# Scaling V by a sum of squares, joint tails of a head pair, and the rescaling of x as planned GpSimd work

## The chip, the cores and the metric

The kernel runs on one core of a Trainium2 chip. The metric is the device time of one execution in microseconds: 1048.24 us is the median of three runs of the kernel before (1047.64 to 1049.55). A core has a matmul engine (TensorE, PE in the profile), three engines for elementwise work (VectorE = DVE, ScalarE = ACT, GpSimd = POOL), and a queue that issues DMAs (SyncE = SP). Each engine executes its instructions in the order in which they stand, and waits at one whose inputs or buffers are not ready.

## The reference

Three stages follow each other. The first is causal attention with a decay, over 4 batches, 8 heads, 576 positions and a head size of 64:

```python
scores = scale * np.matmul(q, k.transpose(0, 1, 3, 2))
cum = np.cumsum(np.log(np.clip(f, 0.0001, 1.0)), axis=-1)
decay = cum[:, :, :, None] - cum[:, :, None, :]
scores = np.where(causal, -1000000000.0, scores + decay)
attn = np.exp(scores - np.max(scores, axis=-1, keepdims=True))
attn = attn / (np.sum(attn, axis=-1, keepdims=True) + 1e-09)
attn_out = np.matmul(attn, v)
x = attn_out.transpose(0, 2, 1, 3).reshape(B * S, H * D)   # 2304 x 512
a, b = x @ w_a, x @ w_b                                    # 512 -> 1536
x = a * b @ w_out                                          # 1536 -> 512
h = x @ w_in                                               # 512 -> 2048
g = np.where(h >= 1, h, np.where(h <= -1, 0.0, (h + 1) ** 2 / 4))
return g @ moe2_w_out                                      # 2048 -> 512
```

All inputs and the output are float32.

## The kernel before

Float32 products are built from half-precision pieces. A matrix is scaled by a power of two and split into a high and a low fp16 part (`xh`/`xl` for the activations, `whi`/`wlo` for weights, `vh`/`vl` for V), and a product is three fp16 matmuls (`mm3`, L589 to L591 in the profile). The scale has to keep the high part in range, so each tensor that is split first has its largest magnitude found: a reduction along the row, a transpose on PE, a maximum over the row, masking to the exponent (`top_of`), and a small matmul that spreads the result to all partitions (`spread`).

The program has two phases. **The first phase** is attention for all 16 pairs of heads, with the first group of the second layer for batches 0 to 2 between its steps. It goes in rounds, seven for each pair: score matmuls (`s`), mask and row minimum on DVE (`prob`, `nm`), Exp on ACT, transposes on PE (`tp`), a split of the probabilities on ACT (`th`) and DVE (`tl`), and matmuls with V (`o`). The 576 queries of a head are four blocks of 128 and a tail of 64. Both heads' tails are computed together, in one round, with head 0 on partitions 0 to 63 and head 1 on 64 to 127. At the end of a head its result is divided by its row sum (`z`) and written to `xt`, and at the end of a batch `xpose` transposes `xt` and splits it into `xh` and `xl`.

V of a pair is loaded (`load_v`, tile `vraw`), its largest magnitude per head is found on DVE (`v_max`, tile `mx`), the scales of a group of up to four pairs are spread to `scs` (`v_scale`), and V is scaled and split (`v_split`: ACT writes `vh`, POOL scales `vraw` in place and writes `vl`). Because `o` is V's scale times the result, the row sum is multiplied by it too.

`xh` and `xl` of batch b are written with the smallest V scale known by then, `xsc[:, b]`. When the last V scale is known, batches 0 to 2 are brought to `xsc[:, 3]` by `rescale(b)`: a ratio and eight multiplications of 576 columns, on DVE (L1087 and L1091). They may not run before the matmuls of the second layer's first group have read the batch.

The instructions of the first phase are not issued at once. `Plan` records them with their dependencies, gives each a duration by a table (`cost`), and puts them in order by a list schedule: at each step the engine that can start first takes the ready operation of highest rank, and the ranks come from 20 sweeps forward and backward. Where PE would idle in that plan, matmuls on a constant tile are put in (L1097, `mm<-mask`), which do no work. The recorded operations are then issued, all from L305, with their order kept.

**The second phase** (all lines but L305 in the profile) is the rest of both layers. It is written after the plan in program order, and the framework's own scheduler may put its instructions on an engine between those of the plan. `xpose(3)` and `rescale(0..2)` belong to it. Weights are loaded in 68 units, decoded on ACT, DVE and POOL, and split ahead of their use.

## Time and profile before

| | value |
|---|---|
| median of three runs | 1048.24 us (1047.64 to 1049.55) |
| profiled execution | 1044.85 us, its span 1043.1 us |
| PE busy | 1010.7 us (97%), 6871 matmuls |
| DVE busy | 736.0 us (71%) |
| ACT busy | 600.4 us (58%) |
| POOL busy | 584.7 us (56%) |
| mean granted clock of PE | 0.990 |

The shares are means over both phases, so they say little of either. A stretch of the trace is read from a table of windows: for each, its length, the busy time of PE, of PE's weight loads, DVE, ACT and POOL with the number of instructions in brackets, the clock that PE was granted as a share of the full 2.4 GHz, the busy share of the DMA engines and GB/s. Matmuls overlap each other, so PE's busy time is not its work. The chain of waits goes back from the last instruction to what released each; its rows have a start, a length, an engine, the tile that is written and the line. A row of a group of operations has, after the bar, the busy time in total, the mean of one in ns, and the idle time of the engine just before them with what ended it. An operation of the first phase is told by its tile, since all have line 305.

### The profile page before, as it was taken

To read this page: it belongs to the slowest core of one execution; us is meant where nothing else is said; L and a number is where in the kernel's file an instruction comes from. 1 tells how busy PE (TensorE), PEld (TensorE's weight loads), DVE (VectorE), ACT (ScalarE), POOL (GpSimd) and SP (SyncE) were. 2 spreads that over 40 slices of the span, in tenths; PEclk is the share of its full clock that TensorE was granted. 3 is DMA by queue.
4 is the path that set the end of the run, shared out by engine and by line. 5 is a ranking of instruction groups with operands and counts; after the bars stand their busy time and mean duration, and the time that the engine had idled before them with its cause. 6 is when DMAs were issued, how large, how long until landed. Compare 5 with 4: busy or idle time off the path is not lost.

```text
span 1043.1 us, 18612 instructions
## 1 busy us (share of the span) xinstructions
PE 1010.7 (97%) x6871; PEld 594.1 (57%) x6871; DVE 736.0 (71%) x1761; ACT 600.4 (58%) x1159; POOL 584.7 (56%) x635
## 2 busy tenths in 40 slices
PE   7999999799899999999999999999999999999998
PEld 6787788678764544455454444445554454455554
DVE  7999999887878774564663777984378767744443
ACT  4899788677765444352543445676666546535342
POOL 6698868565177644352553446785377546725221
PEclk8999999899999999999999999999999999999999
DMA  8663544331033121111120211111012102000112
GB/s 248 176 194 113 161 144 134 108 96 54 2 102 98 48 77 41 41 41 41 41 81 1 81 41 41 41 41 41 1 43 80 41 14 68 1 1 1 66 45 74
DMA packets 22060, 72.06 MB, mean 69 GB/s; under 512 B 2776, under 2 KB 5336, under 8 KB 21904
## 3 DMA queue, kind: packets, MB, share of 16 engines
q1 hardware_dynamic: 21968, 70.87, 22.7%
q8 instruction: 54, 0.88, 0.4%
q14 instruction: 38, 0.31, 0.1%
HBM read 60.26 MB, written 5.96 MB: 63 GB/s over the span
## 4 chain that ended last, share of the span: by engine, by line
PE 70%; DVE 19%; ACT 3%; POOL 3%; issue 3%; DMA 2%; SPq 0%; DVEq 0%; ACTq 0%; POOLq 0%
PE mm L589 21%; PE mm L590 20%; PE mm L591 20%; DVE prob L305 3%; DVE tl L305 3%; PE s L305 2%; PE mm L305 2%; PE tp L305 2%; PE o L305 1%; DMA vraw<-in_v_dram 1%; DVE xt L305 1%; DVE xhl L1091 1%; DVE xhl L741 1%; DVE wm L305 1%; DMA y<-y 1%
## 5 line engine op out<-in xcount | busy, mean ns | idle before, releaser
L640 POOL TENSOR_TENSOR al<-tmp 128x460 f16<-128x460 f32 (+2 forms) x134 | 159.7, 1193 | 192.7 <-ACT tmp L637 183.5
L589 PE MATMUL mm<-xhl,whi_in 128*128 128x460 f16 (+2 forms) x752 | 266.4, 355 | 1.2 <-DVE tmp L776 1.2
L591 PE MATMUL mm<-xhl,wlo_in 128*128 128x460 f16 (+2 forms) x752 | 266.5, 355 | 0.0
L590 PE MATMUL mm<-xhl,whi_in 128*128 128x460 f16 (+2 forms) x752 | 266.5, 355 | 0.0
L590 PE MATMUL mm<-al,wdown 128*128 128x460 f16 (+2 forms) x536 | 190.1, 356 | 1.0 <-POOL al L640 1.0
L591 PE MATMUL mm<-ah,wlo_out 128*128 128x460 f16 (+2 forms) x536 | 190.1, 356 | 0.0
L589 PE MATMUL mm<-ah,whi_out 128*128 128x460 f16 (+2 forms) x536 | 178.8, 356 | 0.5 <-DVE tmp L776 0.5
L636 ACT ACTIVATE ah<-tmp 128x460 f16<-128x460 f32 (+2 forms) x134 | 77.7, 580 | 107.2 <-DVE tmp L776 49.4
L590 PEld LDWEIGHTS <-whi_in 128*128 128x128 f16 x752 | 73.6, 98 | 69.5 <-issue 2.0
L591 PEld LDWEIGHTS <-wlo_in 128*128 128x128 f16 x752 | 73.5, 98 | 69.5
L589 PEld LDWEIGHTS <-whi_in 128*128 128x128 f16 x752 | 73.5, 98 | 68.6 <-issue 0.2
L775 ACT ACTIVATE tmp<-tmp,hmid,ihalf 128x460 f32<-128x460 f32 (+1 forms) x80 | 60.9, 761 | 76.6 <-DVE tmp L774 76.5
L518 POOL TENSOR_TENSOR wm<-wm,wr 128x512 int32<-128x512 int32 x58 | 75.8, 1307 | 50.8 <-DVE wm L515 42.6
L776 DVE SCALAR_TENSOR_TENSOR tmp<-mm,hfull,tmp 128x460 f32<-128x460 f32 (+1 forms) x80 | 55.6, 694 | 60.6 <-ACT tmp L775 56.7
L305 ACT ACTIVATE prob<-prob,nm 128x384 f32<-128x384 f32 (+4 forms) x144 | 80.7, 583 | 16.8 <-DVE nm L305 16.1
L591 PEld LDWEIGHTS <-wlo_out 128*128 128x128 f16 x536 | 52.4, 98 | 51.7 <-issue 1.8
L686 DVE SCALAR_TENSOR_TENSOR tmp<-mm,gr,tmp 128x460 f32<-128x460 f32 (+2 forms) x54 | 36.7, 679 | 63.5 <-PE mm L591 56.4
L590 PEld LDWEIGHTS <-wdown 128*128 128x128 f16 x536 | 52.4, 98 | 50.4 <-issue 0.9
L589 PEld LDWEIGHTS <-whi_out 128*128 128x128 f16 x536 | 52.4, 98 | 49.8
L774 DVE TENSOR_SCALAR tmp<-mm,htop,hlow 128x460 f32<-128x460 f32 (+1 forms) x80 | 59.9, 749 | 28.0 <-PE mm L591 26.5
L637 ACT ACTIVATE tmp<-ah 128x460 f32<-128x460 f16 (+2 forms) x134 | 77.6, 579 | 3.0
L725 DVE SCALAR_TENSOR_TENSOR y<-mm,os,y 128x460 f32<-128x460 f32 (+1 forms) x100 | 64.8, 688 | 20.0 <-PE mm L591 19.9
(185 smaller groups left out, 2115.4 us busy)
## 6 DMA issues: line engine op xcount, KB each, us to landing
wraw<-in_w_dram SPq DMA_DIRECT2D x68, 512.0 KB
raw<-in_qk_dram SPq DMA_DIRECT2D x26, 608.0 KB
vraw<-in_v_dram SPq DMA_DIRECT2D x16, 320.0 KB
qk<-q SPq DMA_DIRECT2D x28, 160.0 KB
out_dram<-tmp SPq DMA_DIRECT2D x16, 230.0 KB
cum_d<-xhl SPq DMA_DIRECT2D x1, 1216.0 KB
y<-in_qk_dram SPq DMA_DIRECT2D x2, 608.0 KB
out_dram<-tmp SPq DMA_DIRECT2D x4, 232.0 KB
```

The lines of the kernel that those rows point to most:

```text
L305: getattr(getattr(self.nc, engine), method)(*a, **kw)
L518: nc.gpsimd.tensor_tensor(t, t, r, ALU.add)
L589: nc.tensor.matmul(o, lhsT=wh, rhs=xh, start=first, stop=False)
L590: nc.tensor.matmul(o, lhsT=wd, rhs=xl, start=False, stop=False)
L591: nc.tensor.matmul(o, lhsT=wl, rhs=xh, start=False, stop=last)
L636: nc.scalar.activation(ah, r, AF.Copy, scale=1.0 / LOW)
L637: nc.scalar.activation(spare, ah, AF.Copy, scale=LOW)
L640: after(delay + 1, lambda: nc.gpsimd.tensor_tensor(al, r, spare, ALU.subtract))
L725: nc.vector.scalar_tensor_tensor(ys, o, sc, ys, ALU.mult, ALU.add)
L774: nc.vector.tensor_scalar(t, o, top[:, m], low[:, m], ALU.min, ALU.max)
L775: after(1, lambda: nc.scalar.activation(t, t, AF.Square, scale=ihalf[:, m], bias=mid))
L776: after(2, lambda: nc.vector.scalar_tensor_tensor(r, o, full[:, m], t, ALU.mult, ALU.max))
```

## The change

**V's bound.** `v_max` is one Square on ACT over both heads of a pair, with the sum of the squares of each row as a second output, instead of a maximum on DVE for each head. The square root of a sum of squares is at least the largest magnitude. `top_of` takes the root of the exponent by a shift, which is one more short DVE operation. There is one scale for a pair, so `scs` has half as many columns, `v_split` takes one operation on ACT and one on POOL for both heads, and two constants of the second layer's scales change by a factor of two.

**Tails.** A pair's tail has one operation for `z`, one reciprocal and one multiplication over 128 partitions, since both heads share a scale, and it is written to columns of `xt` that belong to the pair. `xpose` brings it back with 64-column matmuls against halves of the identity into one tile, and splits it in one operation on each engine instead of two. `xt` needs no zeros.

**Rescaling.** `rescale` runs on POOL, is recorded in the plan with everything else, and so its place is chosen by the list schedule. The smallest scale is found in `xscale`.

The core of the diff:

```diff
@@ top_of
+        if squares:
+            nc.vector.tensor_scalar(m2i[0:n], m2i[0:n], 1, 0x3F800000, ALU.logical_shift_right, ALU.bitwise_and)
+            nc.vector.tensor_scalar(m2[0:n], m2[0:n], 2.0 ** 63, None, ALU.mult)
+        else:
+            nc.vector.tensor_scalar(m2i[0:n], m2i[0:n], 0x7F800000, None, ALU.bitwise_and)
@@ v_max
-            vst["mx", p0] = sm_p.tile([P, 2 * NPAIR], F32, name="mx", tag="mx")
-        mx = vst["mx", p0][:, 2 * (pp - p0):2 * (pp - p0) + 2]
-        nc.vector.tensor_reduce(mx, vraws[pp].rearrange("p a c d -> p a (c d)"), axis=AX.X, op=ALU.max,
-                                apply_absolute_value=True)
+            vst["mx", p0] = sm_p.tile([P, NPAIR], F32, name="mx", tag="mx")
+        mx = vst["mx", p0][:, pp - p0:pp - p0 + 1]
+        nc.scalar.activation(junk, vraws[pp].rearrange("p a c d -> p (a c d)"), AF.Square, accum_out=mx)
@@ v_split
-        for a in range(2):
-            nc.scalar.activation(vh[:, a, :, 0:D], t[:, a], AF.Copy, scale=sc[:, a:a + 1])
-            nc.gpsimd.tensor_scalar(t[:, a], t[:, a], sc[:, a:a + 1], 0.0, ALU.mult, ALU.add)
+        nc.scalar.activation(vh[:, :, :, 0:D], t, AF.Copy, scale=sc)
+        nc.gpsimd.tensor_scalar(t, t, sc, 0.0, ALU.mult, ALU.add)
@@ pv_step, the tail of a pair
-            for i in range(2):
-                rows = slice(i * TAIL, (i + 1) * TAIL)
-                nc.vector.tensor_scalar(z[rows], o[rows, D:D + 1], PSC * 1e-9, sc[rows, i:i + 1], ALU.add, ALU.mult)
+            nc.vector.tensor_scalar(z, o[:, D:D + 1], PSC * 1e-9, sc, ALU.add, ALU.mult)
             nc.vector.reciprocal(z, z)
-            for i in range(2):
-                rows = slice(i * TAIL, (i + 1) * TAIL)
-                h = (2 * pp + i) % H
-                nc.vector.tensor_scalar(xt[rows, NCH - 1, h * D:(h + 1) * D], o[rows, 0:D], z[rows], None, ALU.mult)
+            p = pp % NPAIR
+            nc.vector.tensor_scalar(xt[:, NCH - 1, p * D:(p + 1) * D], o[:, 0:D], z, None, ALU.mult)
@@ xpose, the tails
         for kc in range(KC):
-            nc.tensor.transpose(tp[:, kc * P:(kc + 1) * P], xt[:, NCH - 1, kc * P:(kc + 1) * P], ident)
...
+            for i in range(2):
+                rows = slice(i * TAIL, (i + 1) * TAIL)
+                nc.tensor.matmul(tv[rows, kc, :], lhsT=xt[:, NCH - 1, kc * D:(kc + 1) * D], rhs=ident[:, rows], start=True, stop=True)
+        nc.scalar.activation(h[:, :, 512:576], tv, AF.Copy, scale=sb)
+        nc.vector.scalar_tensor_tensor(l[:, :, 512:576], tv, sb, h[:, :, 512:576], ALU.mult, ALU.subtract)
@@ rescale
-        nc.vector.tensor_tensor(r, xsc[:, B - 1:B], xinv[:, b:b + 1], ALU.mult)
+        nc.gpsimd.tensor_tensor(r, xsc[:, B - 1:B], xinv[:, b:b + 1], ALU.mult)
...
-                nc.vector.tensor_scalar(o, o, r, None, ALU.mult)
+                nc.gpsimd.tensor_scalar(o, o, r, 0.0, ALU.mult, ALU.add)
@@ main program, before the plan is ordered and issued
+    xscale(B - 1)
+    for b in range(B - 1):
+        rescale(b)
     with tc.manual_schedule():
         nc.issue()
@@ main program, second phase
-    for b in range(B - 1):
-        after(6 + 8 * b, lambda b=b: rescale(b))
```

Since the list schedule sets the order, the change moves instructions throughout the first phase. Three places are shown, in the built programs' own order.

On ACT at the start, the small operation `wdg` (a diagonal of the first V scale, for the matmul that spreads it) stands in the kernel before ahead of all work on the tables of cumulative sums (`xhl<-y`) and on weights (`wm`, `wr`):

```order
L305 ACTIVATE xt<-xt 64x576
L305 ACTIVATE wdg_152<-ident,w_0_151 2x2
L305 ACTIVATE vh_136<-vraw_148,scs 128x5x64 x2
L305 ACTIVATE wm_186<-wraw_184 128x512
L305 ACTIVATE wr_187<-wraw_184 128x512
L305 CAST xhl<-y 64x1216 x2
L305 ACTIVATE wm_186<-wraw_185 128x512
```

Now the Square (`junk`, `mx`) comes behind the logarithm, and `wdg` stands behind four operations that were after it:

```order
L305 ACTIVATE xt<-xt 64x576
L305 ACTIVATE junk,mx_150<-vraw_149 128x640
L305 CAST xhl<-y 64x1216
L305 ACTIVATE wm_187<-wraw_185 128x512
L305 CAST xhl<-y 64x1216
L305 ACTIVATE wr_188<-wraw_185 128x512
L305 ACTIVATE wdg_153<-ident,w_0_152 1x1
L305 ACTIVATE wm_187<-wraw_186 128x512
```

The matmul that waits for `wdg` has moved in PE's order as well: 29 of 98 matmuls on the constant tile stood ahead of it at the start, and now 50 of 146.

On DVE, where the last V scale has become known, two ratios and the first eight rescales stand in the kernel before between operations of attention (`z` and `xt` are the end of a pair's tail, `tl` the low part of probabilities, `ISA prob` the mask with the row minimum):

```order
L1087 TENSOR_TENSOR ratio_4633<-xsc,xinv 128x1
L1087 TENSOR_TENSOR ratio_4694<-xsc,xinv 128x1
L305 TENSOR_SCALAR z_0_182<-o_169,scs 64x1 x2
L305 ISA prob_133,nm_181<-s_159,mask 128x128
L305 ISA nm_181 128x1
L1091 TENSOR_SCALAR xhl<-xhl,ratio_4633 128x576 x5
L305 RECIPROCAL z_0_182<-z_0_182 128x1
L305 SCALAR_TENSOR_TENSOR tl_168<-tp_150,th_167 128x384
L1091 TENSOR_SCALAR xhl<-xhl,ratio_4633 128x576 x3
L305 TENSOR_SCALAR xt<-o_169,z_0_182 64x64 x2
L305 SCALAR_TENSOR_TENSOR tl_179<-tp_160,th_178 128x512
```

At the same place, the smallest scale, DVE now has only its reduction and reciprocal:

```order
L305 SCALAR_TENSOR_TENSOR tl_169<-tp_151,th_168 128x384
L305 TENSOR_SCALAR z_0_183<-o_170,scs 128x1
L305 SCALAR_TENSOR_TENSOR tl_180<-tp_161,th_179 128x512
L305 RECIPROCAL z_0_183<-z_0_183 128x1
L305 TENSOR_REDUCE xsc<-scs 128x1
L305 TENSOR_SCALAR ot_228<-ot_228 128x1
L305 TENSOR_SCALAR xt<-o_170,z_0_183 128x64
L305 TENSOR_SCALAR os_229<-winv,ot_228 128x2
L305 ISA prob_133,nm_166<-s_160,mask 128x320
L305 ISA nm_166 128x1
L305 RECIPROCAL xinv<-xsc 128x1
```

On POOL, in the stretch between the preparations of two heads (`k`, `q` and `qk` are the copy and the splits of a head, `al` the low part of the second layer's product), the kernel before has no rescale:

```order
L305 TENSOR_TENSOR al_208<-tmp_206,tmp_205 128x288
L305 TENSOR_SCALAR vraw_189<-vraw_189,scs 128x320
L305 TENSOR_SCALAR k_2_130<-raw_156 128x576
L305 TENSOR_TENSOR qk_2_131<-raw_156,k_2_130 64x576
L305 TENSOR_TENSOR q_2_129<-raw_156,q_2_129 64x640
L305 TENSOR_SCALAR vraw_189<-vraw_189,scs 128x320
```

In the changed kernel the longest run of rescales stands there:

```order
L305 TENSOR_TENSOR al_209<-tmp_207,tmp_206 128x288
L305 TENSOR_TENSOR qk_1_129<-raw_175,k_1_128 64x576
L305 TENSOR_SCALAR xhl<-xhl,ratio_230 128x576 x5
L305 TENSOR_SCALAR xhl<-xhl,ratio_231 128x576
L305 TENSOR_TENSOR ratio_230<-xsc,xinv 128x1
L305 TENSOR_SCALAR xhl<-xhl,ratio_231 128x576 x5
L305 TENSOR_TENSOR al_213<-tmp_211,tmp_210 128x288
L305 TENSOR_SCALAR k_2_131<-raw_157 128x576
L305 TENSOR_TENSOR q_2_130<-raw_157,q_2_130 64x640
```

Five more rescales are spread over rows ahead of these, and the last eight stand behind the last `qk` of the phase. From the last recorded operation on, the order of POOL and SP is that of the kernel before but for four places on POOL.

## Rows read from the trace of the kernel before

**Rows 1.** Windows: us, busy (count) of PE, PEld, DVE, ACT, POOL, clock, DMA, GB/s

```profile
18.00:30.00 12.00, 12.00 (x48) 8.29 (x48) 7.03 (x23) 7.64 (x14) 2.55 (x2) 0.57 0.84 246
30.00:180.00 150.00, 144.07 (x1755) 119.77 (x1752) 145.83 (x494) 130.99 (x281) 121.17 (x116) 1.00 0.52 151
180.00:210.00 30.00, 24.45 (x283) 20.69 (x282) 26.11 (x81) 20.85 (x45) 19.20 (x18) 0.89 0.37 113
210.00:220.00 10.00, 7.77 (x54) 6.00 (x53) 10.00 (x28) 7.06 (x16) 5.11 (x6) 0.83 0.27 80
220.00:258.00 38.00, 37.16 (x454) 30.77 (x453) 28.91 (x93) 29.91 (x65) 23.61 (x23) 1.00 0.28 77
345.00:600.00 255.00, 255.00 (x1317) 127.45 (x1315) 150.46 (x272) 107.80 (x200) 117.74 (x106) 1.00 0.17 50
```

**Rows 2.** Chain of waits, 182 to 215 us: start us, us, what

```profile
182.52 0.92 DVE ratio L1087 x2
184.13 2.17 DVE xhl L1091 x5
186.82 3.31 DVE xhl L1091 x3
...
212.69 1.88 DVE xhl L1091 x3
```

**Rows 3.** Waits of PE, 178 to 224 us: total us, times, longest us

```profile
PE o L305 <- DVE xt L305: 3.3, 1, 3.3
```

**Rows 4.** Groups of operations, DVE: busy us, mean ns, idle us before

```profile
L305 DVE TENSOR_REDUCE mx<-vraw 128x2 f32<-128x640 f32 x16 | 12.9, 809 | 3.7 <-DMA vraw<-in_v_dram 3.7
...
L1091 DVE TENSOR_SCALAR xhl<-xhl,ratio 128x576 f16<-128x576 f16 x24 | 11.9, 538 | 0.0
...
L305 DVE TENSOR_SCALAR xt<-o,z 64x64 f32<-64x64 f32 x32 | 9.0, 280 | 0.4
...
L305 DVE TENSOR_SCALAR z<-o,scs 64x1 f32<-64x1 f32 x32 | 6.9, 215 | 1.9 <-PE o L305 1.5
...
L305 DVE SCALAR_TENSOR_TENSOR xhl<-tp,xsc,xhl 64x256 f16<-64x256 f32 x6 | 2.9, 482 | 0.8 <-ACT xhl L305 0.7
...
L1087 DVE TENSOR_TENSOR ratio<-xsc,xinv 128x1 f32<-128x1 f32 x3 | 1.1, 406 | 0.0
```

**Rows 5.** Timeline of PE, 6 to 25 us: start us, us

```profile
6.62 6.79 PE L1097 MATMUL mm<-mask 128*128 128x224 bf16 x69
17.83 6.47 PE L305 MATMUL s<-y 66*128 66x128 f32 x14 [4.43 <-DMA y<-y]
```

**Rows 6.** Timeline of ACT, 8 to 11 us

```profile
8.18 0.68 ACT L305 ACTIVATE wm<-wraw 128x512 f32<-128x512 f32 x1
...
9.31 1.20 ACT L305 CAST xhl<-y 64x1216 fp32r<-64x1216 f32 x1
```

**Rows 7.** Groups of operations, ACT

```profile
L305 ACT CAST q<-raw 128x640 fp32r<-128x640 f32 x26 | 18.7, 721 | 1.7 <-PE s L305 1.4 <-DMA raw<-in_qk_dram 0.2
L305 ACT ACTIVATE vh<-vraw,scs 128x320 f16<-128x320 f32 x32 | 17.7, 559 | 1.8 <-DVE scs L305 1.4 <-PE o L305 0.4
...
L305 ACT ACT_TABLE_LOAD x2 | 2.6, 1283 | 0.8 <-PEq L1226 0.7
```

**Rows 8.** Groups of operations, POOL

```profile
L305 POOL TENSOR_SCALAR vraw<-vraw,scs 128x320 f32<-128x320 f32 x32 | 18.5, 579 | 27.2 <-ACT vh L305 24.1 <-PE tp L305 2.7
L305 POOL TENSOR_SCALAR k<-raw 128x576 fp32r<-128x576 f32 x26 | 18.4, 707 | 22.4 <-PE s L305 14.7 <-issue 7.2 <-POOL q L305 0.4
```

**Rows 9.** Line 1091: duration ns min/median/max, first and last start us

```profile
L1091 DVE TENSOR_SCALAR xhl<-xhl,ratio x24: 351/361/1637, 184.0 to 265.4; 128x576 f16<-128x576 f16 x24
```

**Rows 10.** Window 205 to 262 us

```profile
205.00:262.00 57.00, 53.93 (x608) 44.52 (x607) 47.62 (x150) 44.18 (x95) 32.57 (x30) 0.97 0.27 76
```

**Rows 11.** Timeline of POOL, 281 us, with the idle time before

```profile
281.06 1.36 POOL L532 TENSOR_SCALAR wm<-wm,wsc 128x512 f32<-128x512 f32 x2 [13.64 <-ACT whi_in L531]
```

**Rows 12.** Timeline of PE, 265 us

```profile
265.57 0.93 PE L305 MATMUL tp<-ident,prob 128*128 128x128 f32 x7
```

More of the change, by code (lines that the diff above doesn't have):

```diff
@@ L377, in tile_decay_attention__then__moe__then__moe2 @@
     winv = const.tile([P, NU], F32, name="winv")
-    scs = const.tile([P, B * H], F32, name="scs")
+    scs = const.tile([P, B * NPAIR], F32, name="scs")
+    junk = const.tile([P, 2 * NCH * D], F16, name="junk")
     xsc = const.tile([P, B], F32, name="xsc")
@@ L449, in constants @@
             nc.gpsimd.memset(V(t[64:P, :]), 0.0)
-        nc.gpsimd.memset(xt[:, NCH - 1, :], 0.0)
     def set_of(hh):
@@ L470, in slot, with top_of @@
         return slots[k][split[k] - 1]
-    def top_of(mx, n):
+    def top_of(mx, n, squares=False):
         tp = psum_t()
@@ L660, in out_scale1 @@
             nc.vector.tensor_scalar(t, group1(g)[0], xinv[:, b:b + 1], 2.0 ** 31, ALU.mult, ALU.mult)
-            nc.vector.tensor_scalar(t[:, 0:1], t[:, 0:1], t[:, 1:2], 2.0, ALU.mult, ALU.mult)
+            nc.vector.tensor_scalar(t[:, 0:1], t[:, 0:1], t[:, 1:2], 4.0, ALU.mult, ALU.mult)
             nc.vector.tensor_scalar(o, winv[:, u:u + 2], t[:, 0:1], None, ALU.mult)
@@ L882, in v_scale @@
             return
-        n = 2 * (p1 - p0)
+        n = p1 - p0
         mx = vst.pop(("mx", p0))[:, 0:n]
-        spread(top_of(mx, n), n, None, scs[:, 2 * p0:2 * p1])
+        spread(top_of(mx, n, True), n, None, scs[:, p0:p1])
     def v_split(pp):
-        t, sc = vraws.pop(pp), scs[:, 2 * pp:2 * pp + 2]
+        t, sc = vraws.pop(pp), scs[:, pp:pp + 1]
         vh, vl = vhs[pp % 2], vls[pp % 2]
-        for a in range(2):
-            nc.scalar.activation(vh[:, a, :, 0:D], t[:, a], AF.Copy, scale=sc[:, a:a + 1])
-            nc.gpsimd.tensor_scalar(t[:, a], t[:, a], sc[:, a:a + 1], 0.0, ALU.mult, ALU.add)
+        nc.scalar.activation(vh[:, :, :, 0:D], t, AF.Copy, scale=sc)
+        nc.gpsimd.tensor_scalar(t, t, sc, 0.0, ALU.mult, ALU.add)
         nc.gpsimd.tensor_tensor(vl, t, vh[:, :, :, 0:D], ALU.subtract)
@@ L995, in pv_step @@
                 z = sm_p.tile([P, NCH - 1], F32, name="z", tag="z")
-                nc.vector.tensor_scalar(z, o[:, :, D], PSC * 1e-9, sc[:, a:a + 1], ALU.add, ALU.mult)
+                nc.vector.tensor_scalar(z, o[:, :, D], PSC * 1e-9, sc, ALU.add, ALU.mult)
                 nc.vector.reciprocal(z, z)
@@ L1060, in round_step, with xscale @@
             pv_step(k - OFF[2])
+    def xscale(b):
+        sb = xsc[:, b:b + 1]
+        nc.vector.tensor_reduce(sb, scs[:, 0:NPAIR * (b + 1)], axis=AX.X, op=ALU.min)
+        nc.vector.reciprocal(xinv[:, b:b + 1], sb)
     def xpose(b):
         sb = xsc[:, b:b + 1]
-        nc.vector.tensor_reduce(sb, scs[:, 0:H * (b + 1)], axis=AX.X, op=ALU.min)
-        nc.vector.reciprocal(xinv[:, b:b + 1], sb)
         h, l = (a[:, :, b * S:(b + 1) * S] for a in (xh, xl))
@@ L1073, in xpose @@
         tp = psum_t()
+        tv = tp[:, 0:KC * TAIL].rearrange("p (k t) -> p k t", k=KC)
         for kc in range(KC):
-            nc.tensor.transpose(tp[:, kc * P:(kc + 1) * P], xt[:, NCH - 1, kc * P:(kc + 1) * P], ident)
-        tv = tp.rearrange("p (k t) -> p k t", k=KC)
-        for i in range(2):
-            rows = slice(i * D, (i + 1) * D)
-            cols = slice(i * TAIL, (i + 1) * TAIL)
-            nc.scalar.activation(h[rows, :, 512:576], tv[rows, :, cols], AF.Copy, scale=sb[rows])
-            nc.vector.scalar_tensor_tensor(l[rows, :, 512:576], tv[rows, :, cols], sb[rows], h[rows, :, 512:576],
-                                           ALU.mult, ALU.subtract)
+            for i in range(2):
[3 more added lines that the diff above has]
+        nc.vector.scalar_tensor_tensor(l[:, :, 512:576], tv, sb, h[:, :, 512:576], ALU.mult, ALU.subtract)
     def rescale(b):
         r = const2.tile([P, 1], F32, name="ratio", tag="ratio")
-        nc.vector.tensor_tensor(r, xsc[:, B - 1:B], xinv[:, b:b + 1], ALU.mult)
+        nc.gpsimd.tensor_tensor(r, xsc[:, B - 1:B], xinv[:, b:b + 1], ALU.mult)
         for a in (xh, xl):
@@ L1138, in tile_decay_attention__then__moe__then__moe2 @@
             if k // RB < B:
+                xscale(k // RB - 1)
                 xpose(k // RB - 1)
```

3 lines of the change are left out of this document (1 added, 2 removed).

## The prediction

> **What bounds the kernel now.** I read the table of stages first, then the chain of waits through the stage that loses most, then who PE waited for there, then the durations of the operations that the change touches. The reader is to see three things.
>
> First, from 345 us on PE is busy all the time (255.00 of 255 us in [rows 1]). The second phase is matmul work, 438 POOL rows and 77 SP rows follow the last planned row in both orders, and they differ in four places and in none. So what the change is worth is what it moves the end of the first phase by, at about 281 us; everything behind shifts along.
>
> Second, in the first phase DVE is the engine that is never free: 145.83 of 150 us from 30 to 180 us, and 10.00 of 10 from 210 to 220, where ACT has 130.99 of 150 and POOL 121.17. PE is "busy" 144.07 there, but its matmuls overlap, so that is no proof of a full engine.
>
> Third, the worst places are two blocks of rescaling on DVE. They belong to the second phase, but stand in DVE's queue in the middle of the first. The chain of waits runs through two ratios (0.92 us), then five and three rescales (2.17 and 3.31 us) before it comes back to PE, and again at 212 us [rows 2]. PE waited 3.3 us in one piece for the DVE operation behind the first block [rows 3]. After that wait the granted clock is down: 0.89 of full speed on average from 180 to 210 us, 0.83 from 210 to 220, against 1.00 before and after [rows 1].
>
> **Term A, the rescaling leaves DVE.** In the order of the changed kernel no rescale stands on DVE; all 24 are on POOL, in places that the list schedule chose. What this block cost is read on PE: from 180 to 210 us it was idle for 30 - 24.45 = 5.55 us, and at 0.89 of the clock lost 24.45 x 0.11 = 2.7 us; from 210 to 220 us, 10 - 7.77 = 2.23 us and 7.77 x 0.17 = 1.3 us. Sum 11.8 us, and I take all of it: A = -11.8. The ends: 0, if what was late behind DVE is late behind POOL instead; and -18, if DVE itself is the limit (24 x 538 ns = 12.9 us [rows 4], 1.1 us of ratios, 4.0 us of clock).
>
> **Term B, the start.** PE ran out of filler matmuls at 13.4 us (69 of them in 6.79 us, 0.098 us each) and stood still for 4.43 us until the rows with the cumulative sums had landed at 17.83 us [rows 5]. From 18 to 30 us the clock was 0.57, near the lower of its two levels (1.2 GHz), with PE busy throughout: 12 x 0.43 = 5.2 us of work lost [rows 1]. The new order has 146 fillers ahead of the first score matmul instead of 98 (27, 23 and 96 instead of 21, 8 and 69), so the wait is covered and the clock should stay up. But they may end too late: the small matmul that the last 96 follow now waits for an ACT operation that stands behind two casts of 1.20 us and two decoding operations of 0.68 us [rows 6], so it comes at about 6.6 + 3.8 = 10.4 us, and 96 x 0.098 = 9.4 us more end at 19.8, 2.0 us after the data. (The same loads stand ahead of those rows in SP's queue, in another order, so I leave 17.8 us.) B lies between -5.2 and +2.0; their sum is -3.2, and as DVE was busy for 7.03 us of that stage and the steps of a round wait for each other, I take -2.0.
>
> **Term C, the rest of DVE's relief.** The maxima go to ACT: 11 of the 16 stand behind the start, 11 x 809 ns = 8.9 us. The tails of a pair are scaled in one operation instead of two: 16 x 215 ns = 3.4 us and 16 x 280 ns = 4.5 us; three of six splits of transposed tails go, 1.4 us [rows 4]. Added is one short operation in each of five scale groups, at most 5 x 215 ns = 1.1 us. That frees 17.1 us of an engine that is 97% busy. What PE can make of it is less: it idles for 5.93 us from 30 to 180 us, and runs 81 fillers there (7.9 us), so 13.8 us at most, and nothing if ACT is next. The order has 48 fillers behind the start instead of 85; 37 x 0.098 = 3.6 us is my value: C = -3.6.
>
> **Term D, what is added.** ACT: 16 squares over 640 columns with a sum; no row shows one with a sum. Bounds: not below the 721 ns of a 640-column cast, not above two 320-column operations (1118 ns) [rows 7]. I take 721, the row of the same width, so 7.9 us for the 11 behind the start. Joining 32 scalings of 320 columns (17.9 us) into 16 of 640, between 721 and 1118 ns, at 830 ns gives 4.6 back, and three splits of tails 1.4. Net ACT +2 us. POOL: 24 rescales of 576 columns. The nearest row is the copy of k, as wide, at 707 ns [rows 8]: 17.0 us; joining the scalings of V gives some 5 back; net +12 us. Its ends are the 351 ns of the same operation on DVE and its 1637 ns at worst [rows 9]. What hides it: POOL idles for 57 - 32.57 = 24.4 us from 205 to 262 us [rows 10], where 16 of them go (11.3 us), and for 13.64 us before 281 us [rows 11], where the last eight go (5.7 us). If that cover fails, all 12 us and ACT's 2 us are on the path. PE: 32 matmuls of 64 columns for 16 transposes; the spacing of transposes is 0.93 / 7 = 0.13 us [rows 12], so between 0 (half as long each) and +2.1 us; I take 1.0. Of the 14 us on ACT and POOL I let 2 show, since queues are in order and the plan's gaps are not the chip's. D = +3.0, between 0 and +16.
>
> The rows say that a rescale is twice as long on POOL (707 against a median of 361 ns). The Trainium skill says the same more strongly: VectorE: DVE Perf Modes, Rules for kernel authors, wants 16-bit operations with a scalar from and to SBUF on VectorE for its fastest mode, and GPSIMD Engine Reference, Engine selection, sends elementwise work to VectorE. By that rule the move costs 24 x 0.346 = 8.3 us of engine time and the sum would be -14.4 + 8.3 = -6.1; by the chain of waits, DVE's time at that place is the dear one. No row of this kernel shows a rescale on POOL.
>
> **The sum.** -11.8 - 2.0 - 3.6 + 3.0 = -14.4 us. The profiled execution took 1044.85 us (span 1043.1), so 1030.45; the median of the runs, 1048.24, is 3.39 above that execution, which gives 1033.8, rounded to 1034.
>
> **Rivals.**
> 1. Half of it comes back (20%). The block's place on the chain is taken by POOL's preparation of the next head or by ACT. For it: behind 220 us POOL, ACT and PE are all between 62 and 98% busy and DVE is no longer full (28.91 of 38) [rows 1]. Against it: the wait of 3.3 us and the clock behind it have no other cause in the rows. A halves to -5.9, B is 0, C halves to -1.8, D stays: -4.7, so 1043.5.
> 2. Slower (9%). The list schedule puts 11 rescales and a ratio in one run on POOL, ahead of a subtraction for the second layer and of the copy and splits of the next head. If they take 1.10 us each, as the three did on DVE while POOL worked (3.31 / 3 [rows 2]), and if score matmuls wait for all 16, that is 17.6 us on the chain, and PE's idling would take the clock down again for 4.0 us: -11.8 - 2.0 - 3.6 + 1.0 + 21.6 = +5.2, so 1053.4. It decides from 16.4 us of such delay on. For it: POOL releases q and k for PE. Against it: 24.4 us of idle time in that very stretch. GPSIMD Engine Reference, Key points, in the Trainium skill, states that GpSimd shares its SBUF interfaces with VectorE and contends with some of its instructions; the spread of 351 to 1637 ns on DVE agrees [rows 9].
> 3. Larger (13%). DVE's 97% was the true limit of the whole first phase and the start keeps its clock without delay: -11.8 - 5.2 - 10 + 2.0 = -25, so 1023.2. For it: no other engine is as full from 30 to 180 us. Against it: PE and ACT have only 6 and 19 us of slack there [rows 1].
> 4. It doesn't do what it says (3%): Square needs another table than Exp and each group of maxima loads two. ACT_TABLE_LOAD takes 1283 ns [rows 7]; five groups make 12.8 us and eat the gain, near 1047. The order has two such loads in both kernels, so this is nearly excluded.
>
> The forecast itself holds 55%, with a range of its own from 1027 to 1040.
>
> **The numbers.** A difference of 0.2% (2.1 us, below 1046.1 or above 1050.4) is what a measurement of this kernel can tell. Faster: the forecast, rival 3 and most of rival 1, 85%. Within: the rest of rival 1 and rival 4, 5%. Slower: rival 2 with a little for what I haven't seen, 10%. The range from 1020 to 1046 covers the forecast, rivals 1 and 3 but for their outer ends, and leaves out rivals 2 and 4.
>
> **What would show it.** Right: PE idles for under 2 us between 175 and 215 us and its clock stays at 1.00 there; from 18 to 30 us the clock is well above 0.57; the first score matmul starts between 17.5 and 20 us; DVE is busy for about 700 instead of 736 us, POOL for about 597, ACT for about 603; the first phase ends near 267 us. Wrong: PE or ACT waits in pieces of 2 us or more for POOL's copy or splits of q and k while rescales run; a rescale takes over 1.1 us; or the first phase ends earlier but PE then waits for weights before 345 us, so that the gain is given back.

## The result and the profile after

The changed kernel takes 1034.74 us (median of four runs, 1033.59 to 1035.86), the kernel before, in the same session, 1048.89 us (1047.64 to 1049.72). The ratio is 0.986, its 95% interval 0.982 to 0.990. The profiled execution took 1033.59 us, its span is 1031.8 us, 11.3 us less than that of before. Runs over 1.5% above the fastest of the same kernel are left out of the ratios here and below, which concerns one of the 11 with the longer filler (1051.57 us) and two of the 13 of the kernel before beside the first group.

The windows of the changed kernel, same columns as [rows 1] and with the same stretches but the first of 18 to 30 us:

```profile
18.00:30.00 12.00, 12.00 (x93) 10.29 (x92) 4.48 (x14) 6.49 (x13) 1.39 (x3) 1.00 0.84 231
30.00:180.00 150.00, 142.04 (x1751) 116.97 (x1750) 139.79 (x477) 136.19 (x297) 123.99 (x108) 0.99 0.54 163
180.00:210.00 30.00, 29.97 (x359) 25.45 (x357) 22.74 (x79) 24.37 (x53) 22.98 (x25) 1.00 0.37 110
210.00:220.00 10.00, 9.89 (x122) 7.91 (x121) 5.63 (x22) 7.32 (x18) 9.84 (x12) 1.00 0.44 145
345.00:600.00 255.00, 253.73 (x1309) 126.64 (x1307) 148.29 (x274) 107.59 (x201) 116.68 (x106) 1.00 0.15 46
```

From 180 to 220 us PE idles for 0.14 us where it idled for 7.78, at full clock; this is what term A said. From 18 to 30 us the clock is 1.00 instead of 0.57. From 30 to 180 us ACT now has 136.19 of 150 us where it had 130.99, and DVE 139.79 where it had 145.83, but PE is not busier. In the second phase PE misses 1.27 us of 255 that it didn't miss before; the one wait listed there is for ACT:

```profile
PE mm L593 <- ACT ah L640: 1.3, 1, 1.3
```

PE's waits from 178 to 224 us, where [rows 3] had 3.3 us, are down to one short one. In the chain of waits (start, length, engine, tile) PE follows PE where [rows 2] went through ratios and the first rescales. From 210.8 to 215.7 us, where [rows 2] had the second block, the chain goes through ACT, but PE lost little by it (9.89 of 10 us busy from 210 to 220 us). The wait first, then two stretches of the chain:

```profile
PE tp L305 <- DVE w L305: 0.3, 1, 0.3
```

```profile
182.28 0.60 PE o L305 x30
182.88 0.84 PE mm L305 x6
183.72 1.40 PE s L305 x11
185.61 0.91 PE o L305 x30
...
210.79 0.71 ACT q L305
...
214.50 0.79 ACT prob L305 x2
```

The rescales on POOL, the joined scaling of V, and on ACT the Square with the instruction that reads its sum (busy us, mean ns, idle before), beside [rows 4, 7, 8]:

```profile
L305 POOL TENSOR_SCALAR xhl<-xhl,ratio 128x576 f16<-128x576 f16 x24 | 17.5, 742 | 2.7 <-PE mm L305 2.7
L305 POOL TENSOR_SCALAR vraw<-vraw,scs 128x640 f32<-128x640 f32 x16 | 13.7, 855 | 17.0 <-ACT vh L305 9.5 <-issue 3.6 <-DVE nm L305 3.3
L305 ACT ACTIVATE vh<-vraw,scs 128x640 f16<-128x640 f32 x16 | 13.3, 833 | 0.9 <-PE o L305 0.6 <-POOL al L305 0.2
L305 ACT ACTIVATE junk<-vraw 128x640 f16<-128x640 f32 x16 | 11.8, 736 | 3.4 <-DMA vraw<-in_v_dram 3.4
...
L305 ACT ACTIVATION_READ_ACCUMULATOR junk<-vraw 128x1 f32 x16 | 3.1, 196 | 0.0
```

A rescale takes 742 ns on POOL (707 was taken), and at most 747. The Square takes 736 ns as the row of a cast said, but an instruction of its own reads the sum for another 196 ns.

PE's start, beside [rows 5]:

```profile
1.47 5.18 PE L1096 MATMUL mm<-mask 128*128 128x224 bf16 x27 [1.47 <-DVE mm L1095]
...
12.52 0.16 PE L305 MATMUL tp<-wdg,ones 1*128 1x1 bf16 x1 [3.56 <-ACT wdg L305]
12.61 11.03 PE L1096 MATMUL mm<-mask 128*128 128x224 bf16 x96
23.48 2.99 PE L305 MATMUL s<-y 66*128 66x512 f32 x12
```

The first score matmul starts at 23.48 us, 5.65 us later than before and behind the 17.5 to 20 of the forecast, for two reasons. The small matmul on `wdg` came at 12.5 us instead of 10.4, as ACT waited 2.28 us for POOL and 0.96 us for DVE ahead of its two casts. And after PE's wait of 3.56 us the clock fell to 0.50, so the 96 fillers took 11.03 us instead of 9.4 (the first row is a window of 2.5 us, the second of 2):

```profile
13.50:16.00 2.50, 2.50 (x15) 1.98 (x14) 2.06 (x4) 1.08 (x3) 2.07 (x3) 0.50 1.06 231
16.00:18.00 2.00, 2.00 (x19) 1.82 (x18) 0.00 (x0) 1.22 (x3) 2.00 (x3) 0.82 0.98 213
```

In the execution without rescaling, with the same order of PE, `wdg` came at 11.41 us, the 96 fillers took 9.37 us and the first score matmul started at 20.71 us.

How far each execution had come is read from matmuls issued by a time, those on the constant tile left out. I worked them out from windows that begin at 0, once of all and once of that tile. Executions with the same first phase can be compared row by row; the two kernels differ by a few small matmuls per batch and in the order of the others, so across them the counts are rough. "None" is without the rescaling, "twice" with each rescale issued twice.

| matmuls issued by (us) | 30 | 60 | 120 | 180 | 220 | 280 |
|---|---|---|---|---|---|---|
| before | 50 | 400 | 1011 | 1719 | 2052 | 2747 |
| changed | 35 | 396 | 1056 | 1738 | 2214 | 2901 |
| rescaling back on DVE | 57 | 363 | 1056 | 1731 | 2160 | 2851 |
| changed, none | 72 | 416 | 1068 | 1743 | 2220 | 2907 |
| changed, twice | 57 | 401 | 1058 | 1733 | 2209 | 2735 |
| before, none | 34 | 313 | 950 | 1605 | 2076 | 2774 |
| before, on GpSimd | 51 | 319 | 969 | 1634 | 2022 | 2698 |
| before, longer filler | 82 | 448 | 1040 | 1768 | 2109 | 2784 |
| longer filler, none | 98 | 455 | 1051 | 1773 | 2233 | 2882 |

At 180 us the two kernels are level (1719 and 1738, 1.6 us at 12 matmuls a us, the changed kernel's rate from 180 to 220 us: 476 in 40). From 180 to 220 us the one before issues 333.

The second phase, by its first and last matmul on the line of the low parts (before, then changed):

```profile
L590 PE MATMUL mm<-xhl,whi_in x752: 286/358/368, 281.0 to 1028.3; 128*128 128x460 f16 x144, 128*128 128x464 f16 x36, 128*128 128x288 f16 x8
```

```profile
L594 PE MATMUL mm<-xhl,whi_in x752: 285/358/368, 268.0 to 1017.4; 128*128 128x460 f16 x144, 128*128 128x464 f16 x36, 128*128 128x288 f16 x8
```

It starts 13.0 us earlier and ends 10.9 us earlier: 2.1 us are given back behind the first phase; the wait of 1.3 us for `ah` above is new there. PE did not wait longer for weights before 345 us: its waits from the end of the first phase to there sum to 1.5 us, against 1.3 before.

### The profile page after: what moved, and what is told of

It is laid out like the page before. It is cut to its first block, busy times and chain, and to the rows that moved or that the text cites. A ratio compares the mean times of both kernels' runs of the same rounds, so it can differ in the third digit from the quotient of the medians.

```text
span 1031.8 us, 18669 instructions
## 1 busy us (share of the span) xinstructions
PE 1007.3 (98%) x6931; PEld 591.3 (57%) x6931; DVE 704.7 (68%) x1687; ACT 602.0 (58%) x1171; POOL 593.7 (58%) x645
## 4 chain that ended last, share of the span: by engine, by line
PE 72%; DVE 14%; ACT 7%; POOL 3%; issue 3%; DMA 1%; DVEq 0%; POOLq 0%; ACTq 0%
PE mm L593 20%; PE mm L594 19%; PE mm L595 19%; PE mm L305 4%; PE tp L305 3%; PE s L305 3%; PE o L305 2%; ACT prob L305 1%; DVE tl L305 1%; ACT th L305 1%; DVE y L729 1%; DVE wm L519 1%; PE mm L1096 1%; DVE prob L305 1%; DVE wm L515 1%
## 5 line engine op out<-in xcount | busy, mean ns | idle before, releaser
L305 ACT ACTIVATE prob<-prob,nm 128x256 f32<-128x256 f32 (+3 forms) x144 | 79.9, 585 | 13.9 <-DVE nm L305 13.8
```

The costliest lines, as they stand in the source:

```text
L305: getattr(getattr(self.nc, engine), method)(*a, **kw)
```

## The experiments

Theory 1: the two blocks of rescales on DVE cost what [rows 1] shows behind 180 us, and the list schedule's places on GpSimd cost little. Theory 2: the gain is DVE's relief and the new plan as a whole. A third question came with the results: what the start is worth. The four kernels of the first group ran on one chip, with the kernel before beside them; so did the two of the second group with the short filler and the maximum on DVE, and the remaining four. Ratios are to the kernel before on the same chip.

### The rescaling in the changed plan

All four keep the plan of the changed kernel word for word; only the 27 operations of the rescaling (`marked`) are touched, where the plan is issued:

```diff
 # back on DVE: not issued with the plan, but in the second phase as before
+            if i in self.marked:
+                continue
...
+    for b in range(B - 1):
+        after(6 + 8 * b, lambda b=b: rescale_late(b))      # on nc.vector
 # same place, on DVE
+            if i in self.marked:
+                self.on_vector(*self.ops[i][1:3])    # the same operation on nc.vector
+                continue
...
 # none: left out
+            if i in self.marked:
+                continue
...
 # twice
+            if i in self.marked and self.ops[i][1] == "tensor_scalar":
+                self.nc.gpsimd.tensor_scalar(*self.ops[i][2])
```

> The plan of the changed kernel is kept word for word on PE and ACT; only the 24 rescales and their ratios are taken out of it and put back on DVE in program order of the second phase, as in the kernel before. In the built order they stand on DVE right behind the last V scale again, eight of them in one block. Theory 1 (the blocks on DVE cost what the profile of before showed, 11.8 us): about 1046, and again PE idles for 4 us or more between 180 and 220 us with a granted clock below 0.95 there. Theory 2 (the gain is DVE's relief by the V bound and the tails, and the new plan as a whole): at most 4 us above the changed kernel, 1035 to 1039, and no such stall. The counts of matmuls by time speak for theory 1: at 180 us both kernels stood at 268 transposes of probabilities, at 220 us the changed one was 9 transposes and 162 matmuls ahead.

> All engines' orders are those of the changed kernel, but each of the 24 rescales (and ratios) is issued to DVE instead of GpSimd at the very place in the global order that the list schedule gave it. It parts the engine from the place. If the place is what counts (spread out, in gaps, not in blocks), the time stays within 2 us of the changed kernel's 1034.7. If the engine is what counts, the waits for the second layer's matmuls and DVE's queue come back: 24 x 0.36 us = 8.7 us of DVE work at least, up to 24 x 1.1 = 26 us where GpSimd holds it up, and the time is 1040 or more. I expect something between, about +4 us (1039), since DVE was busy for 28.4 of 40 us from 180 to 220 us and the rescales add 5.8 us there at 0.36 us each (16 of them), but they bring DVE to wait for PE (the write must come behind the matmuls that read the batch).

> The changed kernel without any rescaling (24 multiplications and three ratios are left out, so batches 0 to 2 keep their own scale and the output is wrong where scales differ); everything else word for word. It prices what the rescaling still costs on GpSimd. Theory (hidden in GpSimd's idle time): within 1 us of the changed kernel, 1033.7 to 1035.7, though 18 us of GpSimd work are gone. Rival (GpSimd's queue releases PE late, or GpSimd holds VectorE up): 4 us or more faster, 1030 or less.

> The changed kernel with each rescale issued twice on GpSimd (so the ratio is applied twice and the output is wrong where it isn't 1); the plan knows nothing of the second ones. Another 24 x 0.74 = 17.8 us of GpSimd work, 11.9 of it between 184 and 224 us, where GpSimd idles for about 5 us, and 5.9 us between 248 and 255 us, ahead of 12 us in which it idles. Theory (the cover is real but used up in the first of these stretches): +2 to +6 us, 1037 to 1041. If GpSimd has more slack than its idle time shows: within 1 us. If each microsecond there is on the path: +12 us and more, 1047, with PE waiting for the copy and splits of q and k.

| | median us (runs) | ratio to before |
|---|---|---|
| back on DVE | 1038.73 (1037.57 to 1039.96) | 0.9873 (0.983 to 0.9917) |
| same place, DVE | 1035.99 (1033.62 to 1037.95) | 0.985 (0.981 to 0.989) |
| none | 1033.43 (1030.9 to 1034.13) | 0.9822 (0.9784 to 0.986) |
| twice on GpSimd | 1048.11 (1045.65 to 1049.73) | 1.0007 (0.9973 to 1.0041) |

Against leaving it out, the rescaling costs 5.3 us in blocks on DVE, 2.6 us in the planned places on DVE, and 1.3 us on GpSimd (the last against a median from another chip; by the ratios GpSimd costs 4.0 us and the planned places on DVE 2.9). In the medians the blocks are the dearest, and of the planned places it isn't shown which engine is cheaper: the intervals overlap. In one execution of each the first phase ends at 267.3 us without rescaling, 268.0 on GpSimd, 271.1 in the planned places on DVE and 274.2 in blocks. The 1039 that I expected of the planned places on DVE was wrong: they are within 2 us of the changed kernel, so by its own mark the place counts more than the engine. For leaving the rescaling out, the runs don't tell "hidden" (within 1 us) from the 4 us of its rival. My expectation of 1046 for the first was wrong too: here the blocks cost half of what they cost in the profile of before. In its windows from 180 to 220 us PE idles for 2.24 us, and the clock does not fall:

```profile
180.00:210.00 30.00, 27.99 (x338) 22.97 (x335) 26.22 (x95) 22.26 (x50) 17.34 (x15) 1.00 0.37 108
210.00:220.00 10.00, 9.77 (x99) 8.24 (x97) 6.14 (x22) 8.40 (x19) 8.79 (x8) 1.00 0.34 96
```

A part of why the same block was so much dearer before shows when DVE and POOL are laid side by side. First the timeline of DVE in the kernel before, then POOL's, then DVE's and POOL's with the block back in the changed plan:

```profile
186.75 3.38 DVE L1091 TENSOR_SCALAR xhl<-xhl,ratio 128x576 f16<-128x576 f16 x3
190.05 0.57 DVE L305 TENSOR_SCALAR xt<-o,z 64x64 f32<-64x64 f32 x2
```

```profile
186.78 1.71 POOL L305 TENSOR_TENSOR q<-raw,q 64x640 fp32r<-64x640 f32 x1
188.57 1.39 POOL L305 TENSOR_TENSOR qk<-raw,k 64x576 fp32r<-64x576 f32 x1
```

```profile
186.66 2.50 DVE L1095 TENSOR_SCALAR xhl<-xhl,ratio 128x576 f16<-128x576 f16 x7
```

```profile
185.94 0.97 POOL L310 TENSOR_TENSOR al<-tmp,tmp 128x288 f16<-128x288 f32 x1 [1.83 <-issue]
188.30 0.71 POOL L310 TENSOR_SCALAR k<-raw 128x576 fp32r<-128x576 f32 x1 [1.39 <-DMA raw<-in_qk_dram]
```

Three rescales took 3.38 us while POOL had two operations with two inputs in a row, and ended within 0.2 us of the second; seven took 2.50 us where POOL was idle from 186.9 to 188.3 us. With the longer filler (below) the same three took 2.93 us beside the same two operations of POOL. The Trainium skill, GPSIMD Engine Reference, Key points, states that GpSimd shares its SBUF interfaces with VectorE and contends with VectorE's instructions in a 2-port mode or with two SBUF inputs; the rows agree that DVE is held up beside GpSimd, and don't show in which mode the rescales ran. All 24 rescales took 538 ns each in the kernel before and 381 back on DVE, 3.8 us in all. The difference in price is 6.8 us (12.1, as measured below, against 5.3); that the hold-up and the clock behind it make all of it is not shown, since the two plans also differ elsewhere.

Doubling costs 14.7 us against none and 13.4 against the changed kernel, where I had expected 2 to 6. GpSimd's cover is used up by 17.8 us more, and PE's longest waits from 220 to 285 us are for POOL:

```profile
PE mm L310 <- POOL al L310: 9.3, 2, 5.6
PE s L310 <- POOL qk L310: 2.5, 1, 2.5
```

### The rescaling in the plan of before

```diff
 # none
-    for b in range(B - 1):
-        after(6 + 8 * b, lambda b=b: rescale(b))
 # on GpSimd, in program order
-                nc.vector.tensor_scalar(o, o, r, None, ALU.mult)
+                nc.gpsimd.tensor_scalar(o, o, r, 0.0, ALU.mult, ALU.add)
```

> The kernel before without its rescaling (24 multiplications and three ratios are left out of DVE's queue, so the output is wrong where the scales of the batches differ); all else word for word. It prices the rescaling in the kernel before, as leaving it out of the changed kernel priced it there (-1.3 us), and putting it back on DVE there (+4.0 us). Theory 1 (in the kernel before the two blocks cost the 11.8 us that its profile shows): about 1037, a gain of 10 to 14 us. Theory 2 (the block is dear only by about 4 us in either kernel, and the stall and the lowered clock of the profile of before come from DVE being late there anyway): 1043 to 1047, and PE still idles for 4 us or more between 180 and 220 us. By the run with the rescaling back on DVE I hold theory 2 for the likelier.

> The kernel before with the rescaling on GpSimd in program order: PE, ACT and SP word for word, DVE without the 27 operations, GpSimd with three runs of eight, the first two of them ahead of the copies and splits of q and k of the next heads. The engine is changed, the place isn't planned. If the engine is what matters, it is within 2 us of the kernel before without rescaling. If the place matters on GpSimd (rival 2 of the prediction), each run of eight takes 8 x 0.74 = 5.9 us ahead of a head's preparation, PE waits for the splits of q and k in pieces of 2 us or more, and it is 5 us or more slower than without rescaling, near or above the kernel before.

Without rescaling: 1041.09 us (1032.64 to 1043.78), ratio 0.9894 (0.983 to 0.9958). On GpSimd unplanned: 1050.65 us (1048.22 to 1058.2), ratio 1.0007 (0.9979 to 1.0035). So the engine alone gains nothing: in one execution the first eight rescales, in a row but for one copy, delay an addition of the weight decode on POOL, ACT waits 5.8 us for it, and PE's clock is down again. The waits, then the window of PE:

```profile
ACT wr L305 <- POOL wm L305: 5.8, 1, 5.8
DVE tl L305 <- ACT th L305: 5.1, 3, 4.2
```

```profile
210.00:220.00 10.00, 7.37 (x52) 6.33 (x52) 4.98 (x15) 6.63 (x14) 6.70 (x7) 0.66 0.32 104
```

The median without rescaling fits neither theory, and the table of matmuls says why: in the profiled execution it is 114 matmuls behind the kernel before at 180 us, before any rescale could matter, and from 180 to 280 us it issues 1169 against 1028, 141 more, near 12 us at 12 a us. The two effects hid each other. What put it behind goes with the clock at the start, with the same order of PE as before [rows 1, 5]:

```profile
18.00:30.00 12.00, 12.00 (x31) 8.12 (x31) 8.09 (x22) 7.29 (x13) 2.14 (x2) 0.50 0.86 242
30.00:45.00 15.00, 15.00 (x92) 9.87 (x91) 9.18 (x35) 8.05 (x18) 4.08 (x6) 0.51 0.25 84
```

### The start

In the changed plan the longest filler was cut (56 of 96 matmuls dropped). In the plan of before it was made longer by 42, with and without rescaling:

```diff
 # changed kernel: at most KEEP = 40 in a run
+                run += 1
+                if run <= KEEP:
+                    self.heat()
...
 # before: 111 instead of 69
+                for _ in range(1 + MORE * (run == 69)):   # MORE = 42
+                    self.heat()
```

> The changed kernel, its order word for word, but a run of matmuls on the constant tile has at most 40: of the 96 ahead of the first score matmul 56 are dropped. The first score matmul then starts with its data, near 18 us instead of 20.7 to 23.5 us. If the late start is on the path, the time falls by 3 to 5 us, to 1030 or 1032. If the start's delay is taken up later (in four runs with the same order PE stood between 35 and 72 matmuls at 30 us and between 1054 and 1068 at 120 us), the time is within 1 us of the changed kernel's.

> The kernel before, word for word, but with 42 more matmuls on the constant tile ahead of the first score matmul (111 in the longest run instead of 69, at 0.098 us each 4.1 us more, which covers the 3.4 to 4.4 us for which PE stood still there). It does the one thing at the start that the changed kernel does as a by-product. Theory (the kernel before loses its clock behind that wait, for 10 us in one of the three profiles with this start and for 25 us in the other two, and this is why its runs spread from 1038.7 to 1056.6): full clock from 18 us on, a median 3 to 9 us below the kernel before, 1041 to 1047, and a spread of its runs of 4 us instead of 10 or more. Rival (what is lost at the start is taken up later, since other engines hold the first phase up): within 2 us of the kernel before, and its spread stays.

> The same, and the rescaling left out (the output is wrong where the batches' scales differ). Against the run with the longer filler alone it prices the two blocks on DVE in the kernel before without the noise of the start. Theory (term A): 10 to 13 us faster than that run, as the matmuls issued between 180 and 280 us showed (1028 with the rescaling, 1169 without, 141 matmuls at about 12 per us). Rival (the blocks cost what they cost in the changed plan, 4.0 us): 3 to 6 us faster.

| | median us (runs) | ratio to before |
|---|---|---|
| changed, short filler | 1031.70 (1028.92 to 1032.71) | 0.9817 (0.9782 to 0.9853) |
| before, longer filler | 1039.15 (1034.75 to 1051.57) | 0.9897 (0.9865 to 0.9929) |
| longer filler, no rescaling | 1027.03 (1025.89 to 1030.08) | 0.9787 (0.9744 to 0.9831) |

The longer filler alone is worth 10.7 us in the median, more than I had expected. In its profile the clock is 1.00 from 18 to 45 us, and PE did not wait for the data:

```profile
7.31 10.81 PE L1103 MATMUL mm<-mask 128*128 128x224 bf16 x111
17.95 4.06 PE L311 MATMUL s<-y 66*128 66x128 f32 x14
```

Its runs still spread over 14 us (1034.75 to 1048.76), so that part of the expectation failed. The spread goes with the clock: the mean granted clock of a run was 0.996 to 0.998 in the eight up to 1040.97 us, and 0.985 to 0.989 in the three above 1043 us; where those three lost it no profile shows. At 180 us it still stalls as before, with a wait of 2.8 us and the clock at 0.89 up to 210 us:

```profile
PE o L311 <- DVE xt L311: 2.8, 1, 2.8
```

Without the rescaling this goes and 12.1 us with it (11.5 by the ratios). That is theory 1 for the kernel before. The window with the longer filler, then the same without the rescaling:

```profile
180.00:210.00 30.00, 24.50 (x263) 21.13 (x263) 26.79 (x79) 20.40 (x44) 19.04 (x18) 0.89 0.32 92
```

```profile
180.00:210.00 30.00, 29.88 (x343) 25.44 (x342) 28.47 (x88) 27.26 (x59) 24.89 (x23) 1.00 0.41 127
```

In these two executions the first phase ends at 276.5 and 264.1 us, 12.4 us apart.

In the changed kernel the shorter filler lets the first score matmul start at 19.65 us, with 1.49 us of waiting for its data. The median falls by 3.0 us; the ratios (0.9817 and 0.986) have overlapping intervals, so a gain is likely and not shown. Five executions of the uncut order stand between 35 and 72 matmuls at 30 us and between 1054 and 1068 at 120 us: most of a late start is made up.

### V's bound, and another plan

```diff
 # largest magnitude on DVE, in the place of the Square
+            if "accum_out" in kw:
+                self.nc.vector.tensor_reduce(kw["accum_out"], a[1], axis=AX.X, op=ALU.max, apply_absolute_value=True)
+                continue
...
-            nc.vector.tensor_scalar(m2[0:n], m2[0:n], 2.0 ** 63, None, ALU.mult)
+            nc.vector.tensor_scalar(m2[0:n], m2[0:n], 2.0 ** 66, None, ALU.mult)
 # the list schedule's cost of a Square with a sum
+            sums = 185.0 * ("accum_out" in args)
```

> The changed kernel, its plan word for word, but the bound of V is again a largest magnitude, found on DVE (16 reductions of 640 columns, about 0.81 us each, in the places of the 16 Squares, which leave ACT; the scale's constant is a fixed one, so V's scale may be another power of two). It undoes the part of term C that moves work from DVE to ACT. Term C (DVE's time in the first phase is worth a part of itself): +3 to +9 us, 1038 to 1044, as 11 x 0.81 = 8.9 us come back to DVE. Rival (from 30 to 180 us ACT is as full as DVE in the changed kernel, and at 180 us both kernels stood at 268 transposes): within 1.5 us.

> The changed kernel, but the list schedule is told that a Square with a sum takes 185 ns more on ACT (the separate read of the sum that the trace shows, 180 to 190 ns, 16 times). The instructions are the same, the plan becomes another one: at the start the diagonal of V's first scale stands ahead of the casts again, and 124 matmuls on the constant tile in one run end near the data. It shows how much the plan alone is worth: within 2 us of the changed kernel (1032.7 to 1036.7) if the plan's details don't matter, 3 us or more either way if they do. I expect 1033, as the first score matmul should start near 19.5 us instead of 20.7 to 23.5 us.

> The same plan with at most 105 matmuls on the constant tile in a run, so that the first score matmul starts with its data near 18 us. A version meant to beat both kernels: 1 to 2 us below the run with 124 of them, 1031 to 1032, if the start is on the path there too; the same time if it isn't.

With the maximum on DVE: 1038.45 us (1036.31 to 1040.54), ratio 0.9886 (0.9849 to 0.9922), 3.7 us above the changed kernel (2.7 by the ratios). The intervals overlap, so it is likely and not shown that DVE's time in the first phase is worth this much in this plan, though ACT is nearly as full. If so, the maxima alone (8.9 of the 17.1 us of term C) are worth what term C gave to all of it.

The corrected cost gives 1033.34 us (1029.57 to 1042.68), ratio 0.9857 (0.9803 to 0.991), and with at most 105 fillers 1041.71 us (1031.45 to 1045.27), ratio 0.9912 (0.988 to 0.9945). The second was meant as a better version and is 7 us slower than the changed kernel in the median (5.5 by the ratios, whose intervals just overlap). PE waited 2.8 us for the data in its profile, and the clock stayed at its lower level until past 45 us. But the profile of the first shows the same loss without a wait for data, behind one of 2.11 us for ACT at 23.9 us:

```profile
23.91 0.33 PE L306 MATMUL tp<-ident,prob 128*128 128x128 f32 x1 [2.11 <-ACT prob L306]
24.08 1.48 PE L306 MATMUL s<-y 66*128 66x320 f32 x4
```

```profile
25.00:30.00 5.00, 5.00 (x19) 4.18 (x18) 2.89 (x8) 3.42 (x7) 0.00 (x0) 0.50 0.78 210
30.00:45.00 15.00, 15.00 (x92) 9.68 (x90) 8.53 (x36) 7.22 (x16) 5.61 (x5) 0.50 0.46 121
```

That profile is of the slowest of the first one's five runs. So one and the same built kernel can hold or lose about 10 us with the clock: from 1029.57 us at a mean granted clock of 0.999 to 1042.68 us at 0.987. The 11 runs of the second go from 1031.45 us at 0.997 to 1045.27 us at 0.984.

## Why the prediction was right, step by step

The time came out within 1 us of the forecast. Its largest term was right, with its mechanism; that the sum fits as closely is luck, since the others were wrong by several us in opposite directions.

- **What bounds it.** Right: the gain is a first phase that ends earlier, by 13.0 us. Not quite: the second phase did not simply shift along, it became 2.1 us longer.
- **Term A, -11.8.** Right, and the mechanism with it. In the kernel before with a warm start, leaving the rescaling out is worth 12.1 us; what GpSimd then costs is 1.3 us by the medians and 4.0 by the ratios, so -8 to -11 net. The end of 0 (late behind POOL instead) happens when the places are not planned: 1050.65 us. What the term did not weigh is that POOL held DVE up in that block; in another plan, with POOL quiet beside it, the block costs 5.3 us. The engine counts less than the place: in the planned places the rescaling costs 2.6 us on DVE, too.
- **Term B, -2.0.** The step that failed. I sized it by one profiled execution, in which the lower clock lasted from about 18.6 to 28.8 us, and capped it at -5.2. That execution was faster than all four runs (1044.85 against 1047.64 us and more), and the forecast added the difference to the median without asking where it came from. In two others with that start the lower clock lasted until 43 to 45 us, and a filler that covers the wait is worth 10.7 us in the median. In the changed kernel the clock was up from 18 us on, as said, but it had been down before, under the fillers. That these would end late was said too, but by 2.0 us, where it was 5.7. By 120 us the executions of the same order are level again.
- **Terms C and D, -3.6 and +3.0.** Together -0.6 were forecast. Without rescaling and with a warm start in both, the plan of before takes 1027.03 us and the changed one 1033.43: the rest of the change costs 6.4 us by the medians (3.7 by the ratios, whose intervals overlap). In the profiles (spans 1025.2 and 1031.2) the first phase ends 3.2 us later and the second takes 2.8 us longer. The first score matmul, too, starts 2.8 us later there (20.71 against 17.95 us), so a part may be the start's. If the relief of DVE is worth something within the new plan (3.7 us by the medians), what is lost lies in the plan as a whole, its start with it, or in the 3.1 us of reads of sums that the Square brought. Which operation it is, no run here settles.
- **What was to show it.** DVE is busy for 704.7 us (about 700 was said), POOL for 593.7 (597), ACT for 602.0 (603), and the first phase ends at 268.0 us (267). From 175 to 215 us PE idles for 0.66 us at full clock (under 2 was said). Only the first score matmul was outside what was named.
- **The sum.** -10.7 for the start, -12.1 for the blocks, +1.3 for GpSimd and +6.4 for the rest give -15.1 against -14.2 measured. That they add up proves nothing: they are the steps of one chain of kernels, and the gap of 0.9 us is that between the medians of the kernel before on two chips. The forecast's -14.4 is close because B was 9 us too small and C and D were 7 us too good.
- **Rivals.** The first (half comes back), the third (DVE the limit) and the fourth did not happen; ACT loads its tables twice, as before. The second is a real mechanism at another load: GpSimd's work doubled costs 14.7 us, and its runs of eight in program order take the gain away. In the changed kernel the longest run stood where GpSimd had room: the one wait of PE that is listed from 178 to 224 us is for DVE.

A faster version was sought and not surely found: the short filler's 1031.70 us is the lowest of a complete kernel. What the runs point to was not tried: the plan of before, a filler that covers the wait for the data, and the rescaling planned on GpSimd, near 1027.03 + 1.3 = 1028 us as an estimate from these runs (1031 with the 4.0 of the ratios).

## What to carry to other kernels

Price a block on a full engine by what PE lost behind it, clock included, and then look at what the other engine on the same memory did during that block: here three operations took 3.38 us beside a busy GpSimd, and seven took 2.50 us beside an idle one. Size what the clock costs from several executions, or test it with a longer filler, since one profile may show the short case. When a list schedule replans everything, measure each part with the plan held fixed, or gains and losses of the plan are put down to the part.

## What the runs showed of the hardware

A fast DVE operation can be held up beside several GpSimd operations in a row. In the changed kernel a bound from both sides (`wm<-wm`, 512 float32 columns), 0.42 us in the median of such operations, took 2.55 us, and PE waited 1.74 us for what stood behind it. DVE, then POOL:

```profile
109.09 2.55 DVE L305 TENSOR_SCALAR wm<-wm 128x512 f32<-128x512 f32 x1
```

```profile
107.62 1.76 POOL L305 TENSOR_TENSOR qk<-raw,k 64x576 fp32r<-64x576 f32 x1
109.35 1.25 POOL L305 TENSOR_TENSOR wm<-wm,wr 128x512 int32<-128x512 int32 x1
110.57 0.78 POOL L305 TENSOR_TENSOR al<-tmp,tmp 128x288 f16<-128x288 f32 x1
111.35 0.95 POOL L305 TENSOR_SCALAR vraw<-vraw,scs 128x640 f32<-128x640 f32 x1
```

It ended at 111.64 us, 0.3 us behind the last of three two-input operations that followed without a gap. With the short filler the same operation took 2.56 us. So one GpSimd operation does not bound such a delay.

PE at the lower clock (1.2 of 2.4 GHz) can stay there while it is "busy" all the time: 15.00 of 15 us from 30 to 45 us at 0.51 in one execution (the kernel before without rescaling), and 14.96 at 1.00 in another of the same order of PE (the kernel before). In both PE had waited for data and then ran attention's matmuls. In the changed kernel it had waited 3.56 us and then ran fillers: the clock was 0.50 from 13.5 to 16 us and 1.00 from 18 us on.
